# First K tile ahead of wq, x on another queue, larger wq packets, and one output store instead of four, in a decode kernel bound by DMA

## The chip, the cores and the metric

The kernel runs on one core of one Trainium2 chip. The metric is the device time of one execution in microseconds (us). "Span" is the time that the profile of one execution covers; here it is about 1.7 us shorter than the device time.

The engines are PE (matmuls), DVE (vector work), ACT (ScalarE), POOL (GpSimd) and SP, which here issues most of the transfers. A DMA transfer is issued by one instruction and moved in packets, each by one of 16 DMA engines. HBM is the chip's main memory, SBUF the core's own, in 128 partitions. K0 is the K tile of the first head, and so on. A number after L is a line of the kernel.

## The reference, cut to what matters

```python
xn = layernorm(x)                                   # x: 4 x 1 x 576, bf16
# A: attention of one new token on the last 2048 positions of the cache
q = xn @ wq                                         # wq: 576 x 4096; 32 heads of 128
k, v = k_cache[:, :, -2048:], v_cache[:, :, -2048:] # 16 K/V heads, each used by 2 q heads
o = softmax(q k^T / sqrt(128)) v
A = o @ wo                                          # wo: 4096 x 576
# B: an MLP on xn; its output and the residuals are added
out = x + A + B(xn)                                 # B uses w3: 576 x 4608 and w4: 4608 x 576
```

The kernel has to read 87 MB for four output rows, 67 MB of it K and V. (The mixer part of B multiplies by w1 and w2; the kernel doesn't load these, and its result passed the comparison with the reference.)

## The kernel before

SBUF is laid out by pools that are opened one after another. Each pool takes the bytes that its tiles need:

```python
const = ctx.enter_context(tc.tile_pool(name="const", bufs=1))
small = ctx.enter_context(tc.tile_pool(name="small", bufs=2))
kvp = ctx.enter_context(tc.tile_pool(name="kv", bufs=NKV))      # 7 tiles of 16 KB per partition
ktp = ctx.enter_context(tc.tile_pool(name="kt", bufs=3))
ptp = ctx.enter_context(tc.tile_pool(name="pt", bufs=3))
wp = ctx.enter_context(tc.tile_pool(name="w", bufs=1))          # wq, then w3, then w4
wop = ctx.enter_context(tc.tile_pool(name="wo", bufs=2))
...
x_bf = const.tile([B, D], BF16)
nc.sync.dma_start(out=x_bf[:], in_=x2)
wq_main = A_wq[0:KJ * P, :].rearrange("(p j) n -> p j n", j=KJ)
wq_sb = wp.tile([P, KJ * NQ + NQ // 2], BF16, tag="w", name="wq_sb")
for j in range(KJ):                                             # four transfers, 8 KB packets
    nc.sync.dma_start(out=wq_sb[:, j * NQ:(j + 1) * NQ], in_=wq_main[:, j, :])
nc.sync.dma_start(out=wq_sb[:, KJ * NQ:], in_=A_wq[KJ * P:D, :].rearrange("r (e f) -> (r e) f", e=2))
...
# then K0 K1 K2 wo V0 K3 V1 K4 ..., each as soon as one of the 7 kv tiles is free:
nc.sync.dma_start(out=t[:].rearrange("p c d -> p (c d)"),
                  in_=win[:, h].rearrange("b (p c) d -> p b (c d)", c=NC))   # 16 KB packets
...
gT = const.tile([P, NF, B], BF16)
def acc_matmuls(lhsT, rhs):                                     # B = 4 output rows per quarter
    for i in range(NQD):
        nc.tensor.matmul(out=acc[i * QD:i * QD + B, :], lhsT=lhsT, rhs=rhs[:, i * CW:(i + 1) * CW],
                         start=False, stop=False, skip_group_check=True)
...
fin = const.tile([P, CW], out.dtype)
nc.vector.tensor_copy(out=fin[:], in_=acc[:])
for i in range(NQD):                                            # four small stores, two on each queue
    eng = nc.sync if i % 2 == 0 else nc.scalar
    eng.dma_start(out=o2[:, i * CW:(i + 1) * CW], in_=fin[i * QD:i * QD + B, :])
```

Of the kernel before, what the change touches and what calls it, by code (L numbers as in the profile page):

```python
# [9 lines left out]
ALU = mybir.AluOpType  # L10
AX = mybir.AxisListType
BF16 = mybir.dt.bfloat16
F32 = mybir.dt.float32
I32 = mybir.dt.int32
PSUM = bass.MemoryType.PSUM

NKV = 7
# [4 lines left out]
def kernel(  # L22
# [14 lines left out]
    nc = tc.nc  # L37
    P = 128
    B, Sq, D = A_x.shape
# [6 lines left out]
    KJ = 4  # L46
    NQ = Hq * Dh
    NF = F // P
# [4 lines left out]
    QD = 32  # L53
    NQD = P // QD
    CG = NC // NQD
    NSL = 4
    SC = NC // NSL
    CW = D // NQD
# [7 lines left out]
    x2 = A_x.flatten_outer_dims()  # L66
    o2 = out.flatten_outer_dims()
# [5 lines left out]
    const = ctx.enter_context(tc.tile_pool(name="const", bufs=1))  # L73
    small = ctx.enter_context(tc.tile_pool(name="small", bufs=2))
    kvp = ctx.enter_context(tc.tile_pool(name="kv", bufs=NKV))
    ktp = ctx.enter_context(tc.tile_pool(name="kt", bufs=3))
    ptp = ctx.enter_context(tc.tile_pool(name="pt", bufs=3))
    wp = ctx.enter_context(tc.tile_pool(name="w", bufs=1))
# [4 lines left out]
    ps_acc = ctx.enter_context(tc.tile_pool(name="ps_acc", bufs=1, space=PSUM))  # L83


    x_bf = const.tile([B, D], BF16)
    nc.sync.dma_start(out=x_bf[:], in_=x2)

    wq_main = A_wq[0:KJ * P, :].rearrange("(p j) n -> p j n", j=KJ)
    wq_sb = wp.tile([P, KJ * NQ + NQ // 2], BF16, tag="w", name="wq_sb")  # L90
    for j in range(KJ):
        nc.sync.dma_start(out=wq_sb[:, j * NQ:(j + 1) * NQ], in_=wq_main[:, j, :])
    nc.sync.dma_start(out=wq_sb[:, KJ * NQ:], in_=A_wq[KJ * P:D, :].rearrange("r (e f) -> (r e) f", e=2))

    w_tiles = {}
    wo_tiles = {}
    kv_tiles = {}
    WOH = 8
    WOR = WOH
# [4 lines left out]
    def load_kv(kind, h):  # L104
        win = k_win if kind == "K" else v_win
        t = kvp.tile([P, NC, Dh], BF16, tag="kv", name=f"{kind.lower()}n")
        nc.sync.dma_start(out=t[:].rearrange("p c d -> p (c d)"),
                          in_=win[:, h].rearrange("b (p c) d -> p b (c d)", c=NC))
        kv_tiles[kind, h] = t

    def load_wo(p):
        t = wop.tile([P, WOR, D], BF16, tag="wo", name="wo_sb")
# [24 lines left out]
    ident_f = const.tile([P, P], F32)  # L137
# [3 lines left out]
    neg_half = const.tile([B, 1], F32)  # L141
    nc.gpsimd.memset(neg_half[:], -0.5)

    AB = ps_acc.tile([P, 512], F32)
    nc.vector.memset(AB[:], 0.0)
    q_ps = AB[:, 0:Hq * B].rearrange("p (h b) -> p h b", b=B)
    g_ps = AB[:, Hq * B:Hq * B + NF * B].rearrange("p (f b) -> p f b", b=B)
    acc = ps_acc.tile([P, CW], F32)
# [18 lines left out]
    def transposed(src_bf, name):  # L167
        dup = small.tile([B, 2, P], BF16, tag="dup")
        nc.vector.memset(dup[:], 0.0)
        for e in range(2):  # L170
            nc.vector.tensor_copy(out=dup[:, e, e:P:2], in_=src_bf[:, KJ * P:D])
        T = const.tile([P, KJ + 2, B], BF16, name=name)
        tp = ps_m.tile([P, KJ + 2, B], BF16, tag="m")
        for j in range(KJ):
            nc.tensor.transpose(out=tp[:, j, :], in_=src_bf[:, j:KJ * P:KJ], identity=ident_bf[0:B, 0:B])
        for e in range(2):
            nc.tensor.transpose(out=tp[:, KJ + e, :], in_=dup[:, e, :], identity=ident_bf[0:B, 0:B])
        nc.vector.tensor_copy(out=T[:], in_=tp[:])
        return T

    xn_f = const.tile([B, D], F32)
    xn_bf = const.tile([B, D], BF16)
    layernorm(xn_f, xn_bf, x_bf)
    xnT = transposed(xn_bf, "xnT")


    for j in range(KJ):
        for h in range(Hq):
            nc.tensor.matmul(out=q_ps[:, h, :], lhsT=wq_sb[:, j * NQ + h * Dh:j * NQ + (h + 1) * Dh],
                             rhs=xnT[:, j, :], start=False, stop=False, skip_group_check=True)  # L190
    for h in range(Hq):
        e, f0 = divmod(h * Dh, NQ // 2)
        nc.tensor.matmul(out=q_ps[:, h, :], lhsT=wq_sb[:, KJ * NQ + f0:KJ * NQ + f0 + Dh],
                         rhs=xnT[:, KJ + e, :], start=False, stop=False, skip_group_check=True)
# [4 lines left out]
    for kb in range(NQD):  # L199
        nc.vector.tensor_copy(out=sel[:, :, :, kb, :],  # L200
                              in_=ident_bf[:].rearrange("p (ib i e) -> p ib e i", ib=2, e=2))
    qs_ps = ps_m.tile([P, 2, 2, Hkv, rep, B], F32, tag="m")
    for ib in range(2):
        for e in range(2):
            nc.tensor.matmul(out=qs_ps[:, ib, e].rearrange("p h r b -> p (h r b)"),
                             lhsT=sel[:, ib, e].rearrange("p k i -> p (k i)"), rhs=q_bf[:], start=True, stop=True)
    qz = const.tile([P, Hkv, 2, 2, NQD, B, rep], BF16)
    nc.gpsimd.memset(qz[:], 0.0)
    for kb in range(NQD):
        for ie in range(4):  # L210
            ib, e = divmod(ie, 2)
            nc.vector.tensor_copy(out=qz[kb * QD:(kb + 1) * QD, :, ib, e, kb, :, :],
                                  in_=qs_ps[kb * QD:(kb + 1) * QD, ib, e].rearrange("p h r b -> p h b r"))
# [17 lines left out]
    own = const.tile([P, WOH], F32)  # L231
    nc.vector.reduce_sum(out=own[:], in_=ident_f[:].rearrange("p (h d) -> p h d", h=WOH), axis=AX.X)

    xsum = const.tile([B, D], F32)
    nc.vector.tensor_tensor(out=xsum[:], in0=xn_f[:], in1=x_bf[:], op=ALU.add)
    for i in range(NQD):
        nc.tensor.matmul(out=acc[i * QD:i * QD + B, :], lhsT=ident_f[0:B, 0:B], rhs=xsum[:, i * CW:(i + 1) * CW],
                         start=False, stop=False, skip_group_check=True)
    ln2_bf = const.tile([B, D], BF16)
    layernorm(None, ln2_bf, xn_bf)  # L240
    ln2T = transposed(ln2_bf, "ln2T")
    gT = const.tile([P, NF, B], BF16)


    def acc_matmuls(lhsT, rhs):
        for i in range(NQD):
            nc.tensor.matmul(out=acc[i * QD:i * QD + B, :], lhsT=lhsT, rhs=rhs[:, i * CW:(i + 1) * CW],  # L247
                             start=False, stop=False, skip_group_check=True)

    kts = {}  # L250
    S_ps = {}
    PT = {}
    O_ps = {}
    st = {}

    def k_transpose(h, s):
        src = kv_tiles["K", h][:].bitcast(I32)[:, s * SC:(s + 1) * SC, :].rearrange("p c (ib i) -> p ib c i", i=QD)
        kt = ktp.tile([P, 2, SC, QD], I32, tag="kt")
        nc.vector.transpose(out=kt[:], in_=src)  # L259
        kts[h, s] = kt  # L260

    def k_mask(h):
        S_ps[h] = ps_s.tile([P, CG, NQD, NJ], F32, tag="S", name="S")
# [81 lines left out]
    def o_pick(h):  # L345
        if h % WOQ < WOQ - 1:
            return
        mk = small.tile([P, WOR, WOH, B], BF16, tag="mk")
        nc.vector.tensor_tensor(out=mk[:], in0=st.pop("R")[:],
                                in1=own[:].unsqueeze(1).unsqueeze(3).to_broadcast([P, WOR, WOH, B]), op=ALU.mult)  # L350
        op = small.tile([P, WOR, B], BF16, tag="op")
        with nc.allow_low_precision("one term is not zero"):
            nc.vector.reduce_sum(out=op[:], in_=mk[:].rearrange("p i h b -> p i b h"), axis=AX.X)
        st["op"] = op

    def o_proj(h):
        if h % WOQ < WOQ - 1:
            return
        op = st.pop("op")
        for i in range(WOR):  # L360
            acc_matmuls(op[:, i, :], wo_tiles[h // WOQ][:, i, :])

# [10 lines left out]
    def mlp_act():  # L373
        xs = const.tile([P, NF, B], F32, name="g_x")
        nc.vector.tensor_copy(out=xs[:], in_=g_ps)  # L375
        u = const.tile([P, NF, B], F32, name="g_u")
        nc.vector.tensor_tensor(out=u[:], in0=xs[:], in1=xs[:], op=ALU.mult)
        nc.vector.tensor_scalar(out=u[:], in0=u[:], scalar1=GELU_A, scalar2=1.0, op0=ALU.mult, op1=ALU.add)
        nc.vector.tensor_tensor(out=u[:], in0=u[:], in1=xs[:], op=ALU.mult)
        nc.scalar.activation(out=u[:], in_=u[:], func=ACT.Tanh, scale=GELU_C)  # L380
        nc.vector.tensor_scalar(out=u[:], in0=u[:], scalar1=0.5, scalar2=0.5, op0=ALU.mult, op1=ALU.add)
        nc.vector.tensor_tensor(out=gT[:], in0=u[:], in1=xs[:], op=ALU.mult)

    def mlp_out(lo, hi):
        w4 = w_tiles["w4"]
# [2 lines left out]


    LAG = 2  # L390
    order = [("K", 0), ("K", 1), ("K", 2)]
    for h in range(Hkv):
        order.append(("V", h))
        if h + 3 < Hkv:
            order.append(("K", h + 3))
    W3_AFTER = ("V", 2)
    pos = {"n": 0, "free": NKV}

    def flush_loads():
        while pos["n"] < len(order) and pos["free"] > 0:  # L400
# [14 lines left out]
    for t in range(Hkv):  # L415
        hm = t - 1
        hv = t - 2
        for s in range(NSL):
            k_transpose(t, s)
            if s == 0:  # L420
                if hm >= 0:
                    sm_max(hm)
                if hv - 1 >= 0:
                    o_norm(hv - 1)
            elif s == 2:
                if hv - 1 >= 0:
                    o_pick(hv - 1)
            if hv >= 0:
                pv(hv, s)
            if s == 0:  # L430
                k_mask(t)
            k_scores(t, s)
            if s == 0:
                if hm >= 0:
                    sm_maxT(hm)
            elif s == 1:
                if hm >= 0:
                    sm_sub(hm)
                    for c4 in range(NQD):
                        sm_exp(hm, c4)  # L440
                if hv - 1 >= 0:
                    o_spread(hv - 1)
            elif s == 3:
                if hv - 1 >= 0:
                    o_proj(hv - 1)
            if t == G_AT:
                mlp_g(s * NF // NSL, (s + 1) * NF // NSL)
                if s == NSL - 1:
                    mlp_act()
        pos["free"] += 1  # L450
        if hv >= 0:
            pos["free"] += 1
        flush_loads()
# [24 lines left out]

    fin = const.tile([P, CW], out.dtype)
    nc.vector.tensor_copy(out=fin[:], in_=acc[:])  # L480
    for i in range(NQD):
        eng = nc.sync if i % 2 == 0 else nc.scalar
        eng.dma_start(out=o2[:, i * CW:(i + 1) * CW], in_=fin[i * QD:i * QD + B, :])


# [28 lines left out]
```

## Time and profile before

| | |
|---|---|
| time, median of the first 3 runs | 216.23 us (216.14 to 216.32) |
| span of the profiled run | 214.6 us |
| busy: PE, DVE, ACT | 56%, 55%, 33% |
| read from HBM | 87.17 MB |

The profile cuts the span into 40 equal slices; a digit is the busy share in tenths. This is the page of the kernel before:

```profile
DMA  5999999999999999999999999999999999999960
GB/s 207 429 437 434 428 429 425 425 425 437 426 429 423 437 431 419 439 425 434 431 428 425 428 428 430 422 434 431 429 418 428 437 419 425 437 427 422 419 262 12
```

The DMA engines are the limit: from the second slice to the 38th they are never under 90% busy. So the time is the start of one unbroken stream, its bytes at its rate, and a tail. The stage windows of the kernel before show the parts. The columns are: stretch and its length in us, busy time of the engines with their instructions, granted PE clock, DMA share, GB/s.

```profile
1.00:2.00 1.00, 0.00 (x0) 0.00 (x0) 0.56 (x2) 0.00 (x0) 0.90 (x5) 1.00 0.02 5
2.00:3.00 1.00, 0.00 (x0) 0.00 (x0) 0.81 (x2) 0.00 (x0) 0.00 (x0) 1.00 0.90 164
3.00:4.00 1.00, 0.00 (x0) 0.00 (x0) 0.34 (x2) 0.00 (x0) 0.45 (x1) 1.00 0.87 360
30.00:190.00 160.00, 96.33 (x2251) 75.84 (x2248) 92.01 (x153) 61.56 (x226) 0.00 (x0) 1.00 1.01 429
208.00:210.00 2.00, 0.77 (x20) 0.56 (x20) 0.00 (x0) 0.00 (x0) 0.00 (x0) 0.69 0.29 116
```

The chain of waits of the kernel before ends in transfers, as it must when DMA is the limit (start, duration in us):

```profile
152.04 30.72 DMA kn<-in_A_k_cache_dram
182.76 0.02 issue
182.78 27.43 DMA w_sb<-in_B_w_dram
```

The timeline of the kernel before, first SP's issues (start and duration in us), then the tail: the matmuls on the last piece of w4, which wait for its landing, then the cast, then the stores.

```profile
0.73 0.36 SPq L87 DMA_DIRECT2D x_bf<-in_A_x_dram  x1
1.16 2.06 SPq L92 DMA_DIRECT2D wq_sb<-in_A_wq_dram  x4
...
210.26 0.65 PE L247 MATMUL acc<-w_sb,gT 128*4 128x144 bf16 x16 [0.61 <-DMA w_sb<-in_B_w_dram]
...
210.96 0.31 DVE L480 CAST fin<-acc 128x144 bf16<-128x144 f32 x1 [5.87 <-PE acc L247]
211.29 0.63 SPq L483 DMA_DIRECT2D out_dram<-fin  x2
211.30 0.92 ACTq L483 DMA_DIRECT2D out_dram<-fin  x2
```

### The profile page before, as it was taken

The page shows a single profiled execution, that of the slowest core. Times are in us where ns is not written, and L with a number is a line of the kernel's source. Part 1 is how long each engine was busy: PE and PEld are TensorE (multiplying, and loading weights), DVE is VectorE, ACT ScalarE, POOL GpSimd, SP SyncE. Part 2 cuts the span into 40 slices and gives each one's busy share as a digit, 9 for nine tenths or more (in the row PEclk, how much of TensorE's full clock was granted, in tenths as well). Part 3 has the DMA queues.
Part 4 walks back from the last instruction along what each step waited for, and adds up shares of the span by engine and source line. Part 5 has one row for each costly group of instructions (what it writes and reads, how often), then busy time and mean ns, then how long its engine had stood idle before and what let it go on. Part 6 is the DMA issues. An engine that isn't in the chain of part 4 may idle for free. (4 is left out here: it accounts for less than half of the span.)

```text
span 214.6 us, 6449 instructions
## 1 busy us (share of the span) xinstructions
PE 121.0 (56%) x2893; PEld 94.9 (44%) x2893; DVE 118.0 (55%) x223; ACT 70.1 (33%) x258; POOL 6.1 (3%) x14
## 2 busy tenths in 40 slices
PE   0461355647470017157999577677474705779752
PEld 0350143445360015145899456555453604557641
DVE  5608799766470047348610798785573924854210
ACT  0000005571634001607070045570725340709600
POOL 5400100000000000000000000000000000000000
PEclk9999999999999999999999999999999999999995
DMA  5999999999999999999999999999999999999960
GB/s 207 429 437 434 428 429 425 425 425 437 426 429 423 437 431 419 439 425 434 431 428 425 428 428 430 422 434 431 429 418 428 437 419 425 437 427 422 419 262 12
DMA packets 7123, 87.58 MB, mean 408 GB/s; under 512 B 820, under 2 KB 824, under 8 KB 1336
## 3 DMA queue, kind: packets, MB, share of 16 engines
q1 hardware_dynamic: 7080, 87.17, 95.7%
q8 instruction: 22, 0.36, 0.6%
q14 instruction: 5, 0.04, 0.0%
q10 hardware_dynamic: 16, 0.00, 0.0%
HBM read 87.17 MB, written 0.00 MB: 406 GB/s over the span
## 5 line engine op out<-in xcount | busy, mean ns | idle before, releaser
L302 ACT ACTIVATE pt<-S 32x128 bf16<-32x128 f32 x256 | 68.5, 268 | 92.0 <-issue 55.3
L259 DVE STREAM_TRANSPOSE kt<-kn 128x1024 int32<-128x1024 int32 x64 | 74.3, 1205 | 11.4 <-DMA kn<-in_A_k_cache_dram 11.4
L313 PE MATMUL O<-pt,vn 128*128 128x8 bf16 x1024 | 37.4, 169 | 43.2 <-DMA vn<-in_A_v_cache_dram 41.7
L313 PEld LDWEIGHTS <-vn 128*128 128x128 bf16 x1024 | 34.4, 105 | 51.3 <-DMA vn<-in_A_v_cache_dram 43.6
L273 PE MATMUL S<-qz,kt 128*128 128x32 bf16 x1024 | 39.1, 189 | 25.2 <-DVE kt L259 25.2
L273 PEld LDWEIGHTS <-kt 128*128 128x128 bf16 x1024 | 33.6, 106 | 36.1 <-DVE kt L259 30.4
L287 DVE TENSOR_REDUCE m<-mxT 8x1 f32<-8x128 f32 x16 | 4.4, 277 | 42.6 <-PE mxT L285 42.6
L316 PE MATMUL O<-pt,ones_bf 128*128 128x64 bf16 x128 | 17.1, 226 | 0.0
L302 ACT ACT_TABLE_LOAD x1 | 1.3, 1283 | 32.6 <-DVE mx L280 32.6
L368 PEld LDWEIGHTS <-w_sb 128*128 128x128 bf16 x144 | 11.4, 164 | 0.5 <-issue 0.4
L368 PE MATMUL AB<-ln2T,w_sb 128*128 128x4 bf16 x144 | 11.5, 202 | 0.0
L280 DVE TENSOR_REDUCE mx<-S 128x8 f32<-128x512 f32 x16 | 10.4, 652 | 1.0 <-PE S L273 1.0
L295 PE MATMUL S<-dg,ones_bf 8*128 8x512 bf16 x16 | 9.6, 601 | 0.1
L265 PE MATMUL S<-negbig,ohT 4*128 4x512 bf16 x16 | 9.6, 601 | 0.0
L316 PEld LDWEIGHTS <-ones_bf 128*128 128x128 bf16 x128 | 8.4, 104 | 0.0
L370 PE MATMUL AB<-ln2T,w_sb 128*128 128x4 bf16 x36 | 7.3, 202 | 0.0
L247 PE MATMUL acc<-w_sb,gT 128*4 128x144 bf16 x144 | 4.8, 294 | 2.8 <-DMA w_sb<-in_B_w_dram 2.8
L324 DVE TENSOR_REDUCE dn<-O 128x8 f32<-128x64 f32 x16 | 3.3, 208 | 5.5 <-PE O L316 5.5
L375 DVE COPY g_x<-AB 128x144 f32<-128x144 f32 x1 | 0.3, 307 | 10.7 <-PE AB L370 10.7
L285 PE MATMUL mxT<-ident_f,mx 128*8 128x128 f32 x16 | 6.0, 374 | 0.3 <-DVE mx L280 0.3
L370 PEld LDWEIGHTS <-w_sb 128*128 128x128 bf16 x36 | 5.9, 165 | 0.0
L247 PEld LDWEIGHTS <-gT 128*4 128x4 bf16 x144 | 3.4, 104 | 3.6 <-issue 3.5
(72 smaller groups left out, 64.9 us busy)
## 6 DMA issues: line engine op xcount, KB each, us to landing
kn<-in_A_k_cache_dram SPq DMA_DIRECT2D x16, 2048.0 KB, 29.3
vn<-in_A_v_cache_dram SPq DMA_DIRECT2D x16, 2048.0 KB, 27.0
wo_sb<-in_A_wo_dram SPq DMA_DIRECT2D x4, 1152.0 KB, 28.8
w_sb<-in_B_w_dram SPq DMA_DIRECT2D x2, 2304.0 KB, 31.8
wq_sb<-in_A_wq_dram SPq DMA_DIRECT2D x4, 1024.0 KB, 4.9
w_sb<-in_B_w_dram SPq DMA_DIRECT2D x3, 1296.0 KB, 32.8
w_sb<-in_B_w_dram SPq DMA_DIRECT2D x2, 576.0 KB, 32.2
w_sb<-in_B_w_dram SPq DMA_DIRECT2D x1, 720.0 KB
```

The lines of the kernel that those rows point to most:

```text
L247: nc.tensor.matmul(out=acc[i * QD:i * QD + B, :], lhsT=lhsT, rhs=rhs[:, i * CW:(i + 1) * CW], start=False, stop=False, skip_group_check=True)
L259: nc.vector.transpose(out=kt[:], in_=src)
L265: nc.tensor.matmul(out=S_ps[h][:].rearrange("p g k j -> p (g k) j"), lhsT=ohT[:], rhs=nb, start=True, stop=False, skip_group_check=True)
L273: nc.tensor.matmul(out=S_ps[h][:, s * (SC // NQD) + g].rearrange("p k j -> p (k j)"), lhsT=kt[:, ib, g * NQD:(g + 1) * NQD, e:2 * QD:2].re ...
L280: nc.vector.reduce_max(out=mx[:], in_=S_ps[h][:].rearrange("p g k j -> p j (g k)"), axis=AX.X)
L285: nc.tensor.transpose(out=mxT[:], in_=st[h][:], identity=ident_f[:])
L295: nc.tensor.matmul(out=S_ps[h][:].rearrange("p g k j -> p (g k) j"), lhsT=ones_bf[0:NJ, :], rhs=dg, start=False, stop=False, skip_group_ch ...
L302: nc.scalar.activation(out=PT[h][kb * QD:(kb + 1) * QD, :, c4, :], in_=S_ps[h][c4 * QD:(c4 + 1) * QD, :, kb, :], func=ACT.Exp, scale=scale)
L313: nc.tensor.matmul(out=O_ps[h][:, 0:NJ], lhsT=vn[:, g * NQD + s, :], rhs=pt[:, g, s, :], start=(g == 0 and s == 0), stop=False, skip_group ...
L316: nc.tensor.matmul(out=O_ps[h][:, NJ:].rearrange("p (c j) -> p c j", j=NJ), lhsT=ones_bf[:], rhs=pt[:, g:g + DG, s, :], start=False, stop= ...
L368: nc.tensor.matmul(out=g_ps[:, i, :], lhsT=w3[:, j * F + e * (F // 2) + f0:j * F + (e + 1) * (F // 2):NFH], rhs=ln2T[:, j, :], start=False ...
L370: nc.tensor.matmul(out=g_ps[:, i, :], lhsT=w3[:, KJ * F + f0:KJ * F + F // 2:NFH], rhs=ln2T[:, KJ + e, :], start=False, stop=False, skip_g ...
```

## The change

It had two intents: start the stream sooner and give DVE K0 to transpose while wq is on its way; and store the output by one DMA. For the single store the four batch rows have to be 8 partitions apart, so the matmuls into `acc` write 32 rows, 28 of them from zero columns, and their left operands are padded with zeros.

```diff
-    x_bf = const.tile([B, D], BF16)
-    nc.sync.dma_start(out=x_bf[:], in_=x2)
-    ... (wq: four transfers with 8 KB packets, one with 4 KB)
+    x_bf = const.tile([B, D], BF16)
+    nc.scalar.dma_start(out=x_bf[:], in_=x2)
+    load_kv("K", 0)
+    wq_main = A_wq[0:KJ * P, :].rearrange("(p j) n -> p (j n)", j=KJ)
+    for e in range(2):                              # two transfers, 16 KB packets
+        lo, hi = e * 2 * NQ, (e + 1) * 2 * NQ
+        nc.sync.dma_start(out=wq_sb[:, lo:hi], in_=wq_main[:, lo:hi])
     ... (the 4 KB piece of wq, as before)
+    for s in range(NSL - 1):                        # after the first layernorm
+        k_transpose(0, s)
-    xsum = const.tile([B, D], F32)
+    idz = const.tile([B, QD], F32)                  # zeros, with 1.0 in every 8th column
+    xsum = xn_f
-    gT = const.tile([P, NF, B], BF16)
+    gT = const.tile([P, NF, QD], BF16)
+    nc.gpsimd.memset(gT[:], 0.0)
+    op = const.tile([P, WOR, QD], BF16)             # was a tile of the pool "small"
+    nc.gpsimd.memset(op[:], 0.0)
-            nc.tensor.matmul(out=acc[i * QD:i * QD + B, :], ...
+            nc.tensor.matmul(out=acc[i * QD:(i + 1) * QD, :], ...
     ... (gT and op are written at every 8th column)
-    for i in range(NQD):
-        eng = nc.sync if i % 2 == 0 else nc.scalar
-        eng.dma_start(out=o2[:, i * CW:(i + 1) * CW], in_=fin[i * QD:i * QD + B, :])
+    nc.sync.dma_start(out=o2.rearrange("b (i n) -> i b n", i=NQD), in_=fin[0:P:RS, :])
```

More of the change, by code (lines that the diff above doesn't have):

```diff
@@ L83 @@
     ps_acc = ctx.enter_context(tc.tile_pool(name="ps_acc", bufs=1, space=PSUM))
-    x_bf = const.tile([B, D], BF16)
-    nc.sync.dma_start(out=x_bf[:], in_=x2)
-    wq_main = A_wq[0:KJ * P, :].rearrange("(p j) n -> p j n", j=KJ)
-    wq_sb = wp.tile([P, KJ * NQ + NQ // 2], BF16, tag="w", name="wq_sb")
-    for j in range(KJ):
-        nc.sync.dma_start(out=wq_sb[:, j * NQ:(j + 1) * NQ], in_=wq_main[:, j, :])
-    nc.sync.dma_start(out=wq_sb[:, KJ * NQ:], in_=A_wq[KJ * P:D, :].rearrange("r (e f) -> (r e) f", e=2))
     w_tiles = {}
@@ L109, in load_kv @@
         kv_tiles[kind, h] = t
+    x_bf = const.tile([B, D], BF16)
+    nc.scalar.dma_start(out=x_bf[:], in_=x2)
+    load_kv("K", 0)
+    wq_sb = wp.tile([P, KJ * NQ + NQ // 2], BF16, tag="w", name="wq_sb")
+    wq_main = A_wq[0:KJ * P, :].rearrange("(p j) n -> p (j n)", j=KJ)
+    for e in range(2):
+        lo, hi = e * 2 * NQ, (e + 1) * 2 * NQ
+        nc.sync.dma_start(out=wq_sb[:, lo:hi], in_=wq_main[:, lo:hi])
+    nc.sync.dma_start(out=wq_sb[:, KJ * NQ:], in_=A_wq[KJ * P:D, :].rearrange("r (e f) -> (r e) f", e=2))
     def load_wo(p):
@@ L142 @@
     nc.gpsimd.memset(neg_half[:], -0.5)
+    RS = QD // B
     AB = ps_acc.tile([P, 512], F32)
@@ L184, with k_transpose @@
     xnT = transposed(xn_bf, "xnT")
+    kts = {}
+    def k_transpose(h, s):
+        src = kv_tiles["K", h][:].bitcast(I32)[:, s * SC:(s + 1) * SC, :].rearrange("p c (ib i) -> p ib c i", i=QD)
+        kt = ktp.tile([P, 2, SC, QD], I32, tag="kt")
+        nc.vector.transpose(out=kt[:], in_=src)
+        kts[h, s] = kt
+    for s in range(NSL - 1):
+        k_transpose(0, s)
     for j in range(KJ):
@@ L232 @@
     nc.vector.reduce_sum(out=own[:], in_=ident_f[:].rearrange("p (h d) -> p h d", h=WOH), axis=AX.X)
-    xsum = const.tile([B, D], F32)
+    idz = const.tile([B, QD], F32)
+    nc.gpsimd.memset(idz[:], 0.0)
+    nc.gpsimd.tensor_copy(out=idz[:, 0:QD:RS], in_=ident_f[0:B, 0:B])
+    xsum = xn_f
     nc.vector.tensor_tensor(out=xsum[:], in0=xn_f[:], in1=x_bf[:], op=ALU.add)
     for i in range(NQD):
-        nc.tensor.matmul(out=acc[i * QD:i * QD + B, :], lhsT=ident_f[0:B, 0:B], rhs=xsum[:, i * CW:(i + 1) * CW],
+        nc.tensor.matmul(out=acc[i * QD:(i + 1) * QD, :], lhsT=idz[:], rhs=xsum[:, i * CW:(i + 1) * CW],
                          start=False, stop=False, skip_group_check=True)
@@ L241 @@
     ln2T = transposed(ln2_bf, "ln2T")
-    gT = const.tile([P, NF, B], BF16)
+    gT = const.tile([P, NF, QD], BF16)
+    nc.gpsimd.memset(gT[:], 0.0)
+    op = const.tile([P, WOR, QD], BF16)
+    nc.gpsimd.memset(op[:], 0.0)
     def acc_matmuls(lhsT, rhs):
         for i in range(NQD):
-            nc.tensor.matmul(out=acc[i * QD:i * QD + B, :], lhsT=lhsT, rhs=rhs[:, i * CW:(i + 1) * CW],
+            nc.tensor.matmul(out=acc[i * QD:(i + 1) * QD, :], lhsT=lhsT, rhs=rhs[:, i * CW:(i + 1) * CW],
                              start=False, stop=False, skip_group_check=True)
-    kts = {}
     S_ps = {}
@@ L254 @@
     st = {}
-    def k_transpose(h, s):
-        src = kv_tiles["K", h][:].bitcast(I32)[:, s * SC:(s + 1) * SC, :].rearrange("p c (ib i) -> p ib c i", i=QD)
-        kt = ktp.tile([P, 2, SC, QD], I32, tag="kt")
-        nc.vector.transpose(out=kt[:], in_=src)
-        kts[h, s] = kt
     def k_mask(h):
@@ L350, in o_pick @@
                                 in1=own[:].unsqueeze(1).unsqueeze(3).to_broadcast([P, WOR, WOH, B]), op=ALU.mult)
-        op = small.tile([P, WOR, B], BF16, tag="op")
         with nc.allow_low_precision("one term is not zero"):
-            nc.vector.reduce_sum(out=op[:], in_=mk[:].rearrange("p i h b -> p i b h"), axis=AX.X)
-        st["op"] = op
+            nc.vector.reduce_sum(out=op[:, :, 0:QD:RS], in_=mk[:].rearrange("p i h b -> p i b h"), axis=AX.X)
     def o_proj(h):
@@ L358, in o_proj @@
             return
-        op = st.pop("op")
         for i in range(WOR):
@@ L381, in mlp_act @@
         nc.vector.tensor_scalar(out=u[:], in0=u[:], scalar1=0.5, scalar2=0.5, op0=ALU.mult, op1=ALU.add)
-        nc.vector.tensor_tensor(out=gT[:], in0=u[:], in1=xs[:], op=ALU.mult)
+        nc.vector.tensor_tensor(out=gT[:, :, 0:QD:RS], in0=u[:], in1=xs[:], op=ALU.mult)
     def mlp_out(lo, hi):
@@ L390 @@
     LAG = 2
-    order = [("K", 0), ("K", 1), ("K", 2)]
+    order = [("K", 1), ("K", 2)]
     for h in range(Hkv):
@@ L396 @@
     W3_AFTER = ("V", 2)
-    pos = {"n": 0, "free": NKV}
+    pos = {"n": 0, "free": NKV - 1}
     def flush_loads():
@@ L418 @@
         for s in range(NSL):
-            k_transpose(t, s)
+            if t > 0 or s == NSL - 1:
+                k_transpose(t, s)
             if s == 0:
```

## The prediction

> **What bounds the kernel now.** The DMA stream. The page's slice row shows the DMA engines at 9 tenths or more from the second slice to the 38th, at 417 to 439 GB/s; PE is busy 56%, DVE 55%. The chain of waits ends in three long DMA pieces, the last a 27.4 us wait for the w4 weights until 210.21. So the time is start + bytes at the stream's rate + tail. Stage windows show the ends. Start: no data before 2 us, 164 GB/s in 2 to 3 us, 360 in 3 to 4, then above 400. Tail: from 204 us the rate falls (354, 224, 158, 74 GB/s), as the engines finish unevenly; the last piece lands at 210.21, PE's last 16 matmuls take 0.65, the cast 0.31, output issues run from 211.29 to 212.22 (two on each queue), the span ends at 214.6 (measured time: 1.7 more).
>
> **What the change does.**
> 1. Start: K0 becomes SP's first issue. Today x's issue (0.36 us) stands there, at 0.73, and wq follows at 1.16. The stream starts 0.43 us earlier, and all of it counts. The Trainium skill ("DMA: Bandwidth & Descriptors", section "Issuing engines are not separate DMA queues") says that another issuing engine saves only issue time; that is what I count.
> 2. wq in 16 KB packets: packet records show 309 ns (median) for 8 KB, 611 for 16 KB. 256 pairs over 16 engines save 16 x 7 ns = 0.11 us. The slow first packets (up to 1.4 us) look like start-up, which K0 will pay instead; I count 0.1.
> 3. Order: wq lands 4.9 us later (2 MB at 430 GB/s), about 19 us. The first scores move from 27.5 to about 30. Three of K0's transposes (1.2 us each) fill DVE's present gap of 6.7 us, so head 0 ends near 32.5 instead of 31.5. The V2 load that waits for K0's buffer is issued 1 to 2 us later than 30.88; but loads take 27 to 32 us to land, so the queue holds that much work and doesn't run dry. Worth 0.
> 4. Zero-padded gT, op, idz: 32 output rows instead of 4, the same 144 moving columns; matmuls stay at about 0.3 us, weight loads at 0.1. POOL gains about 1 us of memsets (estimate from qz: 2048 columns, 1.79 us). Off the path.
> 5. Output: one issue instead of two per queue; it should end at 211.6 to 211.8, not 212.22. Saves 0.5 us, on the path. The wait for completion stays: the same page ("Anatomy of one DMA") puts the fixed cost at about 2 us, mostly the write's receipt; here 2.4 us pass from the last issue's end to the span's.
>
> Sum: 0.43 + 0.11 + 0.1 + 0.5 = 1.1 us.
>
> **Predicted: 215.1 us, range 214.3 to 216.0.** Faster by over 2%: 0.02; within 2%: 0.97; slower by over 2%: 0.01.
>
> **What would show each step.** First data near 1.6 us; w4's last piece at 209.6; no slice between the second and 38th under 9 tenths; V2's issue at 32 to 33; cast to span's end 2.8 us instead of 3.3; matmuls into acc unchanged.
>
> **What would make it wrong.** Five engines finish about 3 us behind the rest; they seem to carry the 22 instruction fetches (0.93 us each). One fetch more or less on the slowest moves the end by 0.9 us. A queue run dry between 35 and 50 us, if head 0 ends much later than 33. A single output DMA that completes later. A start-up ramp that belongs to wq's layout would give 0.4 more.

## The result, and the profile after

| | before | after |
|---|---|---|
| time, median of 6 runs | 216.21 us (216.03 to 216.32) | 217.63 us (217.48 to 217.93) |
| ratio | | 1.0067, 95% interval 1.0054 to 1.008 |

A ratio is the mean time of one kernel's fast runs over that of the other's fast runs in the same rounds, so it is not quite the ratio of the medians. Executions over 1.5% slower than the fastest of the same kernel are left out of the means. The kernel became slower by 1.4 us instead of faster by 1.1 us.

The page of the kernel after, and its stage windows:

```profile
DMA  6999999999999999999999999999999999999960
GB/s 244 422 428 438 419 427 426 413 422 431 422 430 419 431 428 418 433 416 422 431 425 425 419 425 420 425 428 416 427 428 415 418 427 431 428 421 415 418 274 28
```

```profile
1.00:2.00 1.00, 0.00 (x0) 0.00 (x0) 0.56 (x2) 0.00 (x0) 0.90 (x5) 1.00 0.02 5
2.00:3.00 1.00, 0.00 (x0) 0.00 (x0) 0.81 (x2) 0.00 (x0) 0.00 (x0) 1.00 0.89 262
3.00:4.00 1.00, 0.00 (x0) 0.00 (x0) 0.34 (x2) 0.00 (x0) 0.46 (x1) 1.00 1.25 524
30.00:190.00 160.00, 96.50 (x2259) 76.24 (x2260) 94.48 (x157) 61.75 (x226) 1.53 (x3) 1.00 1.01 425
208.00:210.00 2.00, 1.30 (x51) 0.86 (x43) 0.00 (x0) 0.00 (x0) 0.00 (x0) 1.00 0.47 194
```

The chain of waits of the kernel after has the same last links, the K transfers 0.75 us longer and the end 1.8 us later:

```profile
153.16 31.47 DMA kn<-in_A_k_cache_dram
184.63 0.01 issue
184.64 27.35 DMA w_sb<-in_B_w_dram
```

The timeline of the kernel after:

```profile
0.73 0.67 SPq L98 DMA_DIRECT2D kn<-in_A_k_cache_dram  x1
1.46 1.04 SPq L109 DMA_DIRECT2D wq_sb<-in_A_wq_dram  x2
...
212.04 0.43 PE L266 MATMUL acc<-w_sb,gT 128*32 128x144 bf16 x16 [0.91 <-DMA w_sb<-in_B_w_dram]
...
212.52 0.31 DVE L490 CAST fin<-acc 128x144 bf16<-128x144 f32 x1 [5.67 <-PE acc L266]
212.85 0.70 SPq L491 DMA_DIRECT2D out_dram<-fin  x1
```

Two things are to be seen. No slice has a gap: the engines are as busy as before, so the queue did not run dry. But in the long stage from 30 to 190 us, where the change touches no load, the same full share moves 425 GB/s instead of 429. This difference alone is worth about 160 x 4 / 429 = 1.5 us. "Busy" only says that a packet was under way; here the packets themselves took longer. The trace's records of single packets show it (source of this table: all 16 KB packets of each run):

```
16 KB packets         before                     after
611 ns                4056 of 4096               411 of 4352
612 to 615 ns         17                         2757 (2132 of them 614)
619 or 621 ns         1                          1059
```

Such a table tells more than a mean: before, practically every packet takes exactly 611 ns. After, about half take 614 and a quarter take 619 or 621. The weights' packets moved alike (medians: 18 KB from 686 to 689 ns, 9 KB from 347 to 351), and so did the 22 instruction fetches of 16 KB (means: 0.94 to 1.07 us). In the first 20 us of the changed kernel, once the start-up is over, packets are still at 611 ns.

So the spans differ by these parts, in us. All but the last column is from the two profiles: the first large packet and the last large packet's end are from the packet records, the others from the timeline.

| part | before | after | difference | predicted |
|---|---|---|---|---|
| span's start to first large packet | 2.15 | 2.18 | +0.03 | -0.43 |
| first to last large packet (the stream) | 207.67 | 209.40 | +1.72 | -0.21 |
| stream's end to the cast | 1.14 | 0.95 | -0.19 | 0 |
| cast's start to the span's end | 3.61 | 3.18 | -0.43 | -0.5 |
| sum (the span) | 214.57 | 215.70 | +1.13 | -1.1 |

### The profile page after: what moved, and what is told of

Read it like the earlier page. It is cut to its first block, busy times and chain, and to the rows that moved or that the text cites. A ratio compares the mean times of both kernels' runs of the same rounds, so it can differ in the third digit from the quotient of the medians.

```text
span 215.7 us, 6448 instructions
## 1 busy us (share of the span) xinstructions
PE 120.5 (56%) x2893; PEld 95.0 (44%) x2893; DVE 119.3 (55%) x223; ACT 70.3 (33%) x258; POOL 8.1 (4%) x18
## 5 line engine op out<-in xcount | busy, mean ns | idle before, releaser
L377 PEld LDWEIGHTS <-w_sb 128*128 128x128 bf16 x144 | 11.4, 163 | 0.5 <-issue 0.4
L202 PE MATMUL AB<-xnT,wq_sb 128*128 128x4 bf16 x128 | 3.7, 166 | 7.4 <-DMA wq_sb<-in_A_wq_dram 7.4
L202 PEld LDWEIGHTS <-wq_sb 128*128 128x128 bf16 x128 | 3.6, 104 | 7.6 <-DMA wq_sb<-in_A_wq_dram 7.6
L266 PE MATMUL acc<-w_sb,gT 128*32 128x144 bf16 x144 | 4.6, 279 | 2.3 <-DMA w_sb<-in_B_w_dram 2.2
```

The lines of the kernel that those rows point to most:

```text
L202: nc.tensor.matmul(out=q_ps[:, h, :], lhsT=wq_sb[:, j * NQ + h * Dh:j * NQ + (h + 1) * Dh], rhs=xnT[:, j, :], start=False, stop=False, ski ...
L377: nc.tensor.matmul(out=g_ps[:, i, :], lhsT=w3[:, j * F + e * (F // 2) + f0:j * F + (e + 1) * (F // 2):NFH], rhs=ln2T[:, j, :], start=False ...
```

## The experiments

The theory was formed from the list of SBUF addresses in the two built programs, which no profile view shows. Each pool takes the bytes that its tiles need, so the start of every later pool depends on the sizes of the tiles in the earlier ones. The change removes the tile xsum (2304 bytes per partition) and two small tiles of op (128), and adds idz (128), a larger gT (2016 more) and op (512). The sum is +224 bytes, and all pools behind move by it:

```
first byte in each partition     before                     after
K and V tile (first of 7)        38144 = 149 x 256          38368 = 149 x 256 + 224
wq / w3 / w4 tile                168192 = 657 x 256         168416 = 657 x 256 + 224
wo tile                          209664 = 819 x 256         209888 = 819 x 256 + 224
```

**Theory placement:** a packet that lands in a tile off a multiple of 256 bytes takes longer. The Trainium skill gives a hint: "DMA: Bandwidth & Descriptors", section "How a descriptor splits into AXI transactions", says of reads that DMA transactions start at 256-byte boundaries, and that a descriptor (one piece of a transfer) that doesn't start on one has a first transaction whose leading bytes are fetched for nothing. **Rival queue:** x on the ScalarE queue, beside SP's, slows the stream. **Rival order:** K0 ahead of wq changes how the engines meet in memory. The outputs are right.

### e1: the changed kernel, back on 256 bytes

```diff
+    pad = const.tile([P, 16], BF16, name="pad")     # 32 bytes
+    nc.gpsimd.memset(pad[:], 0.0)
     x_bf = const.tile([B, D], BF16)
```

> The changed kernel with an unused tile of 32 bytes ahead of the others, so that the K, V, wq, w3, w4 and wo tiles start on a multiple of 256 bytes again (K0 at byte 38400 of the partition instead of 38368). Theory placement (the padded operands moved the tiles off 256 bytes, and each packet into them takes longer): 16 KB packets back at 611 ns (median) instead of 614 to 621, time 215.0 to 215.5, ratio 0.994 to 0.997. Rival queue [...]and rival order (K0 ahead of wq changes how the engines meet): packets stay at 614 to 621 ns, time 217.3 to 217.9, ratio 1.006.

Measured: 215.69 us, before 216.07 (of all before runs of this group), ratio 0.9982 (0.997 to 0.9995). 4190 of the 4352 packets of 16 KB take 611 ns. The 1.4 us loss is a 0.4 us gain, and the long stage is back at 429 GB/s:

```profile
30.00:190.00 160.00, 98.15 (x2288) 77.32 (x2289) 94.50 (x157) 61.58 (x226) 1.47 (x3) 1.00 1.01 429
```

The ratio is a little above the range that I gave, so the placement is not all that the prediction had wrong.

### e2: the kernel before, moved off 256 bytes

```diff
+    pad = const.tile([P, 112], BF16, name="pad")    # 224 bytes
+    nc.gpsimd.memset(pad[:], 0.0)
     x_bf = const.tile([B, D], BF16)
```

> The kernel before with an unused tile of 224 bytes, so that its tiles start where those of the changed kernel do (K0 at byte 38368, 224 past a multiple of 256), and nothing else. Theory placement: 16 KB packets 614 to 621 ns after the first 20 us, time 218.0 to 218.8, ratio 1.008 to 1.012. Rivals queue and order: no effect, 216.2, ratio 1.000.

Measured: 218.32 us, ratio 1.0102 (1.0088 to 1.0115). No load, no matmul and no order was touched, and the kernel lost 2.2 us. Its stage windows give the changed kernel's rate in the long stage:

```profile
30.00:190.00 160.00, 94.40 (x2212) 74.51 (x2209) 91.91 (x152) 61.56 (x226) 0.00 (x0) 1.00 1.01 424
```

Only 9 of its 4096 K and V packets are at 611 ns or under (median of all 614, mean 618.2), and the stream is 209.47 us long instead of 207.67.

### e3: the changed kernel with x on SP again

```diff
-    nc.scalar.dma_start(out=x_bf[:], in_=x2)
+    nc.sync.dma_start(out=x_bf[:], in_=x2)
```

> The changed kernel with x on SP again, ahead of K0; the tiles stay at byte 38368. Theory placement: packets stay slow, time 217.7 to 218.3 (x's issue costs about 0.4 us), ratio 1.007 to 1.010. Rival queue: packets 611 ns, time 215.3 to 215.8, ratio 0.996 to 0.998. Rival order: as theory placement.

Measured: 218.5 us, ratio 1.0111 (1.0096 to 1.0126); packets 614 to 621 ns. The rival "queue" is refuted. The ratio is slightly above the expected range; the reason shows below, in the parts on the last matmuls and on SP's closing stop.

### e4: the output part alone

The edit is the part of the change from `xsum` on, on the kernel before; loads, queues and order are those of before. The tiles land at byte 38368, as in the changed kernel.

> The kernel before with the padded operands and the single output store alone; loads, queues and order as before. Its tiles land at byte 38368 as in the changed kernel. Theory placement: packets slow, stream 2.0 to 2.5 us longer, tail 0.5 shorter, time 217.6 to 218.3, ratio 1.006 to 1.010. Rivals queue and order: packets 611 ns, time 215.6 to 215.9, ratio 0.997 to 0.999.

Measured: 218.21 us, ratio 1.0102 (1.0088 to 1.0116). The rival "order" is refuted as well. The ratio is also the same as that of e2, which has the placement without the new output: the output part itself gave nothing here. That was the second surprise.

### f: which tiles, and which offset

f_kv_only has the pad of 224 bytes, and a second one of 32 bytes in a pool of its own between the K/V pool and the next, so that only the K and V tiles are off 256 bytes.

```diff
+    padp = ctx.enter_context(tc.tile_pool(name="padp", bufs=1))   # behind kvp
+    pad = const.tile([P, 112], BF16, name="pad")
+    pad2 = padp.tile([P, 16], BF16, name="pad2")
```

> The kernel before with K and V tiles at 224 bytes past a multiple of 256 (byte 38368) and, by a second pad of 32 bytes behind them, all other large tiles (transposed K, probabilities, wq, w3, w4, wo) back on a multiple of 256. Theory A (a DMA packet into a tile off 256 bytes takes longer): K and V packets of 16 KB at 614 to 621 ns, weight packets at their old 347, 389 and 686 ns, time 217.4 to 217.9, ratio 1.005 to 1.008. Rival B (the engines' own reads and writes of shifted operands disturb the DMA): all packets at the old durations, 216.1, ratio 1.000.

Measured: 217.55 us, ratio 1.006 (1.0045 to 1.0075); K and V packets at a median of 614 ns. The packets of wo, w3 and w4, whose tiles were back on 256 bytes, kept their old medians of 347, 686 and 389 ns in the same stream. So the loss goes with the tile that a packet lands in, and not with the engines' reads of shifted operands (DVE and PE still read shifted K and V here). The 22 instruction fetches of 16 KB, which are not among these packets, did take longer: 1.05 us on average against 0.93 before; why was not tried.

The other three are the kernel before with a pad of 32, 64 and 128 bytes in place of the 224.

> The kernel before, all large tiles 32 bytes past a multiple of 256 (and of 64). Rule 256 (every start off 256 bytes costs, by the bytes that the first piece wastes: 32 here): a smaller loss than 224 bytes gave, 16 KB packets 612 to 615 ns, time 216.5 to 217.5, ratio 1.002 to 1.006. Rule 64 (a start off 64 bytes costs a fixed amount): as with 224 bytes, 218.3, ratio 1.010.

> The kernel before, all large tiles 64 bytes past a multiple of 256, on a multiple of 64. Rule 256: slower, 16 KB packets above 611 ns, time 217 to 218.3, ratio 1.004 to 1.010. Rule 64: no effect, packets 611 ns, 216.1, ratio 1.000.

> The kernel before, all large tiles 128 bytes past a multiple of 256. Rule 256: slower, packets above 611 ns, time 217 to 218.3, ratio 1.004 to 1.010. Rule 64 (or 128): no effect, packets 611 ns, 216.1, ratio 1.000.

| all large tiles past a multiple of 256 by | ratio to before (95%) | 16 KB packets after 37 us, mean ns |
|---|---|---|
| 0 (the kernel before) | 1 | 613.2 |
| 32 bytes | 1.0101 (1.0084 to 1.0117) | 617.9 |
| 64 bytes | 1.0077 (1.0062 to 1.0092) | 617.3 |
| 128 bytes | 1.0072 (1.0057 to 1.0087) | 616.6 |
| 224 bytes (e2) | 1.0102 (1.0088 to 1.0115) | 618.2 |

All four offsets are slow, so a multiple of 64 or 128 bytes is not enough. I had expected a smaller loss with 32 bytes, because then only 32 bytes of the first transaction are wasted; that was wrong. The loss does not grow with the wasted bytes as the skill's table would have it (that section speaks of reads; here the shifted side is written). The two offsets that are no multiple of 64 cost about 1.0%, the other two about 0.75%. The rule is shown for tiles, and not for every packet: two pieces of w4 start 128 bytes past 256 in the kernel before too (9 and 27 rows of 1152 bytes into the tile), and the 10368-byte packets of the first of them take 389 ns (median) like those of the pieces on either side. Whether that is because they are few (see h3) or because of their size was not tried.

### g: where the rest of the predicted gain went

On 256 bytes, the change gave 0.4 us in e1, and the prediction's sum was 1.1 us. So its parts were run with a pad of 32 bytes on one chip: g0 is e1's kernel again; g1 is the output part alone (e4 with the pad); g2 is g1 with x on the ScalarE queue; g3 is g0 with wq in four transfers of 8 KB packets.

> The changed kernel on 256 bytes once more (it was 0.9982 of before, against a sum of 1.1 us, 0.995), beside its parts on the same chip. Expected again 215.5 to 215.9, ratio 0.997 to 0.999.

> The kernel before with the padded operands and the single output store alone, pad of 32 bytes so that all large tiles are on 256 bytes. If the output part is worth its predicted 0.5 us: 215.5 to 215.8, ratio 0.997 to 0.998. If the start was where the expected gain went, this equals the whole aligned change within 0.2 us; if the output part gives nothing, 216.1, ratio 1.000.

> The last one with x issued on the ScalarE queue as well, so that wq's first transfer is SP's first issue; load order (wq, then K) and 8 KB packets as before. If the earlier start is worth its issue time (0.4 us): 215.1 to 215.4, ratio 0.995 to 0.997, and 0.3 to 0.4 us below the last run. If an earlier start is given back: as the last run. If K0 first costs something of its own, this beats the whole aligned change.

> The aligned changed kernel with wq in 8 KB packets (four transfers of 1 MB) again. If the 16 KB packets are worth their predicted 0.11 us: 0.1 us above the aligned changed kernel, 215.6 to 216.0, ratio 0.998 to 1.000; a difference over 0.3 us either way means the layout of wq's transfers counts for more than its packets.

Then, after the other runs, h1 is g2 with wq in 16 KB packets, still ahead of K0; and h2 is the kernel before with x on the ScalarE queue and nothing else.

```diff
-    nc.sync.dma_start(out=x_bf[:], in_=x2)          # the whole of h2
+    nc.scalar.dma_start(out=x_bf[:], in_=x2)
```

> Padded operands and one output store, 256-byte tiles, x on the ScalarE queue, and wq in 16 KB packets ahead of K0 (two transfers instead of four, so the store's semaphore is again the one that SP's closing waits reach third, as in the changed kernel). If K0's own issue made the start late and the closing waits give the 0.5 us: first large packet at 1.74 us as with wq first in 8 KB, w4 landing at 209.7, landing to span's end 3.7 instead of 4.2; span 213.3 to 213.5, time 215.0 to 215.3, ratio 0.993 to 0.996. If the closing waits have nothing to do with it: landing to end 4.2, time 215.6 to 215.9. If 16 KB packets of wq bring the late start: first packet at 2.17, w4 landing at 210.1.

> The kernel before with x issued on the ScalarE queue, and nothing else. First large packet at 1.74 us instead of 2.15, w4 landing at 209.7 to 209.9, span 214.1 to 214.2; time 215.7 to 215.9, ratio 0.997 to 0.999. If the earlier start is given back on the way: 216.2, ratio 1.000.

| run | first issue on SP | ratio to before (95%) | first large packet | end of stream | cast to end | SP issues |
|---|---|---|---|---|---|---|
| before | x | 1 | 2.15 | 209.82 | 3.61 | 52 |
| g1: output part | x | 0.9998 (0.9983 to 1.0013) | 2.16 | 209.89 | 3.66 | 51 |
| h2: x on ScalarE's queue | wq, 8 KB | 0.9982 (0.9969 to 0.9994) | 1.78 | 209.54 | 3.46 | 51 |
| g2: both | wq, 8 KB | 0.9982 (0.9968 to 0.9997) | 1.74 | 209.32 | 3.72 | 50 |
| g3: all, wq in 8 KB | K0 | 0.9996 (0.9982 to 1.0009) | 2.20 | 209.60 | 3.71 | 50 |
| g0: all (the aligned change) | K0 | 0.997 (0.9955 to 0.9985) | 2.17 | 209.60 | 3.18 | 48 |
| h1: as g0, wq before K0 | wq, 16 KB | 0.9964 (0.9951 to 0.9978) | 1.75 | 209.49 | 3.18 | 48 |

(Times in us, from the profile of one execution of each. SP issues are DMA issues in the program's order on SP.) The table answers four questions.

**The start.** With x out of the way and wq first, the first packets leave 0.4 us sooner, as predicted, and it lasts to the end: h2 gained 0.37 us by its medians. With K0 first there is no gain at the start. The stage windows show it; this is g2:

```profile
1.00:2.00 1.00, 0.00 (x0) 0.00 (x0) 0.56 (x2) 0.00 (x0) 0.87 (x5) 1.00 0.58 95
2.00:3.00 1.00, 0.00 (x0) 0.00 (x0) 0.81 (x2) 0.00 (x0) 0.04 (x2) 1.00 0.67 213
```

and this is g0:

```profile
1.00:2.00 1.00, 0.00 (x0) 0.00 (x0) 0.56 (x2) 0.00 (x0) 0.87 (x5) 1.00 0.02 5
2.00:3.00 1.00, 0.00 (x0) 0.00 (x0) 0.81 (x2) 0.00 (x0) 0.04 (x2) 1.00 0.97 262
```

In both, SP's first issue begins at 0.73 us. From there to the first large packet it is 1.01 us for wq (1.05 in h2) and 1.44 us for K0; in e3, where K0's issue begins at 1.18, it is 1.44 again. So the transfer decides it. The packets' size does not: h1's first transfer is wq in 16 KB packets, and its first large packet leaves at 1.75 us. K0's access pattern has one level more (batch, partition, row), and its issue took 0.67 us; which property of it costs the 0.43 us was not tried. K0 first then wins some of it back: the stream from first to last packet is 207.41 to 207.48 us in three profiles (g3, g0, e1) against 207.58 to 207.77 with wq first (g2, before, g1, h1, h2); why was not tried.

**The packets of wq.** g0 and g3 differ only in them, and their streams end at the same 209.60 us. 16 KB packets of wq are worth nothing that shows. The difference between the two (0.7 us in time, 0.77 in span) lies behind the stream: 0.24 us in the last 16 matmuls (0.43 and 0.67 us), and 0.53 us from the cast's start on.

**The last matmuls.** Their 0.43 or 0.65 us is not a property of the change: with 4-row operands e2 has 0.65 and f_before_pad32 has 0.42; with padded ones g3 has 0.67 and g0 0.43. It goes with the clock that PE was granted. These are the windows of just these matmuls, in the kernel before and in the kernel after; the clock stands in front of the DMA share:

```profile
210.26:210.90 0.64, 0.64 (x16) 0.33 (x15) 0.00 (x0) 0.00 (x0) 0.00 (x0) 0.50 0.00 0
212.04:212.47 0.43, 0.43 (x16) 0.24 (x15) 0.00 (x0) 0.00 (x0) 0.00 (x0) 1.00 0.00 0
```

Of the 14 runs whose trace has clock records, the five with 0.65 or 0.67 us (before, e2, h1, h2, h3) were at 0.50 there, and the nine with 0.42 to 0.47 us at 1.00 (e1, with 0.47, fell to 0.50 partway). g3, e3 and f_before_pad128 have the long form and no clock record. So the 0.19 us between the stream's end and the cast, in the table of parts above, is mostly the clock and not the edit. What decided when the clock fell stays open.

**The output store.** One store is issued in 0.70 us where one of the four took 0.26 to 0.61, and its data lands no sooner: the last completion comes 2.14 us after the cast's start before, and 2.11 us in g0. What differs is what SP does after it. SP checks its semaphores in five instructions, then reports to the other engines. In each run SP stands still once for 0.42 to 0.46 us in this sequence, on nothing that the trace shows. Where it stands depends on the number of DMA issues that SP had made before:

```
SP issues   runs              SP stands still                                  cast to end, us
52          before, e2        after the 3rd check                              3.61, 3.60
51          g1, e4, h2        after the 4th check                              3.66, 3.67, 3.46
50          g2, g3            after the 5th check                              3.72, 3.71
49          e3                after the drain behind the checks                3.60
48          after, g0, e1, h1 after its report to the other engines            3.18 in all four
```

With each issue fewer on SP the stop moves one instruction later, and with 48 it falls behind SP's report, where the others don't wait for it: in g0 GpSimd clears the semaphores meanwhile. h3 below, with 56 issues, fits: SP stands still for 0.45 us four instructions before the place of the kernel before, between its two store issues. So the 0.43 us that the changed kernel gained in the tail were not the saved issues as such: g1 saves one of the two issues per queue and gains nothing. This also explains, with 0.24 us more in the last matmuls, why e3 is slower than the changed kernel by more than x's issue (1.08 us in span, of which the later start is 0.43). A fixed place in the instruction stream would fit a refill of the instruction memory, which the Trainium skill ("Runtime: NRT & Kernel Launch", section "Instruction fetch mechanics") describes as blocks of 256 instructions, mostly hidden; the trace shows no such fetch there, so this is a guess. My expectation for h1 named the order of the semaphores as the reason; e3, whose store's semaphore is also checked third and which has no gain, refutes that form of it.

h1, expected at 215.0 to 215.3 us, came at 215.53: it kept the early first packet and the short close, but the stream was 0.16 us longer than in g2 (one profile of each), and it fell on the long form of the last matmuls. By their intervals h1 and g0 are equal; both beat both kernels.

### h3: when do slow packets begin?

In e2 K and V are slow from the first packet and wq's 8 KB packets are not; in the changed kernel K0, wq and most of K1 are fast and K2 is slow. All these tiles are off 256 bytes alike. h3 is e2 with wq in eight transfers of 4 KB packets (one look; its state is unknown, and its time of 218.74 us is not used).

> The kernel before with tiles 224 bytes past 256 and wq in eight transfers of 4 KB packets. With four transfers of 8 KB packets the slow packets began with K0, after five large transfers (11 to 12 us); in the changed kernel with K2, again after five (19 to 22 us). If the number of transfers or packets decides, wq's later 4 KB packets are already above 159 ns from about 5 to 7 us on. If time or bytes decide, or the source (K and V but not wq), wq stays at 159 ns and K0 is slow from its first packet. No use is made of the time (about 218.5).

Measured: wq's 4 KB packets go from 159 ns to 162 to 165 ns in the middle of wq, from about 8.4 us on. Counted in packets of 4 KB and more, over the whole core, half of the packets are slow near the 570th in h3 (8.5 us), the 580th in e2 (13.2 us) and the 640th in the changed kernel (23 us). That is 36 to 40 per DMA engine, and about five transfers, in all three, while the times and the bytes differ by more than a factor of two. So neither time nor bytes nor the source decides, but a count of packets or of transfers. The trace of f_kv_only tells which packets count. There wq lies on 256 bytes, and K and V stay mostly at 611 ns until half of them are slow near the 1260th large packet of the core (35 us). That is the 490th packet of K and V, and so of those into a tile off 256. So the core's total does not decide either; what counts are the packets (or transfers) into tiles off 256, and the count differs: about 490 there, 570 to 640 in the three runs above, 680 and 740 in f_before_pad64 and f_before_pad128. Why the first ones are spared stays open.

## Why the prediction was wrong

- **What bounds the kernel: right.** The stream stayed unbroken, and the queue did not run dry. V2 was issued at 34.29 us, where 32 to 33 was predicted, and the first scores came at 32.4 us instead of about 30; it did not matter.
- **The step that failed most is step 4: "Zero-padded gT, op, idz ... Off the path."** I costed the padding as engine time (where it held: matmuls into acc stayed at about 0.3 us, and POOL's memsets, 1.9 us instead of about 1, stayed off the path) and not as bytes. The padded tiles moved every later tile by 224 bytes, off 256. This costs 209.60 to 211.57 us at the stream's end in the changed kernel, 1.97 us, and 1.80 us when done to the kernel before alone (209.82 to 211.62). The times agree: 1.0067 became 0.9982 and 0.997 with the pad, and 1 became 1.0102 when the kernel before was moved off 256.
- **Step 1, "The stream starts 0.43 us earlier, and all of it counts": wrong for K0, right for wq.** Measured -0.03 us with K0 first, 0.37 to 0.41 with wq first. The Trainium skill's page ("DMA: Bandwidth & Descriptors", section "Issuing engines are not separate DMA queues") holds: another issuing engine saved the issue time and no more (0.37 to 0.41 us, against 0.43 from x's issue to wq's). My fault was to take the time from issue to first packet as equal for all transfers.
- **Step 2, 16 KB packets: 0.11 us predicted, 0.00 measured** (g0 against g3). With the 0.1 for the start-up, 0.21 us were predicted, and the stream did shorten by 0.24 us in g0. That is luck: it goes with K0 first, and not with the packets.
- **Step 5, "one issue instead of two per queue ... Saves 0.5 us": right in sum by luck, wrong in its mechanism.** The single store lands 0.03 us sooner. The 0.43 us come from SP's stop moving out of the way. The Trainium skill's page "DMA: Bandwidth & Descriptors", section "Anatomy of one DMA — SWDGE (gpsimd) path", gives about 2 us of fixed cost for a DMA issued from GpSimd. SP issued this store, and from its issue to its last completion it is 2.11 - 0.34 = 1.77 us; no run here issued it from GpSimd.
- What would make it wrong: I listed a starved queue, an unlucky fetch, a late store and a ramp. None was it; SBUF addresses were not on the list.

## What to carry to other kernels

When a stream of large DMA packets bounds a kernel, look at the built addresses of its SBUF destinations before and after every change of any tile's size, and try padding a small pool so that large tiles start on a multiple of 256 bytes; here 32 bytes of padding are worth 0.8 to 1.0%. When a stage that the change doesn't touch gets slower at an unchanged busy share, compare the durations of single packets, which busy shares hide. And a gain of half a microsecond at the end can belong to the closing sequence and not to the edit: run the edit alone before crediting it.

## What the Trainium skill lacked or had wrong

- "DMA: Bandwidth & Descriptors", "How a descriptor splits into AXI transactions": it tells the cost of a start off 256 bytes, for reads, as wasted beats that grow with the offset; it has no figure for writes. For 16 KB packets written into SBUF, 32, 64, 128 and 224 bytes off all cost (613.2 ns on 256 bytes; 617.9, 617.3, 616.6 and 618.2 off it), not in proportion to the wasted bytes, and the page's rules for kernel authors don't mention the SBUF start at all. That the cost begins only after some 490 to 740 packets into tiles off 256 is on no page.
- "SBUF — State Buffer", "Operand start alignment": it treats the start of an operand as a matter of legality and says that nothing was timed. For a DMA destination the start is worth 0.7 to 1.0% of this kernel's time.
- No page has the time from the start of an issue to the first packet by access pattern: 1.01 to 1.05 us for wq, 1.44 us for a K tile.
- No page has the stop of 0.42 to 0.46 us in SP's closing sequence, or that its place moves with the number of DMA issues on SP.
